# A decode step's backward pass: two MLP weight gradients and three wq gradients stored by GpSimd in three row pieces each

## The chip, the cores and the metric

The kernel runs on one core of a Trainium2 chip. A core has TensorE (PE, with its weight loads shown apart as PEld), VectorE (DVE), ScalarE (ACT), GpSimd (POOL) and SyncE (SP), and sixteen DMA engines that move data between HBM and SBUF for all of them. The metric is the device time of one execution in microseconds; less is better.

## The reference

One token of a pre-norm decoder block, and its gradients. With `xn = layernorm(x)`, the output is `x + attention(xn) + mlp(xn)`:

```
q = xn @ wq                      # 32 heads of 128; wq is 640 x 4096
p = softmax(q . k_cache / sqrt(128))   # 32 heads, 8192 cached positions
o = p . v_cache ; attention = o @ wo   # wo is 4096 x 640
mlp = (silu(xn @ w1) * (xn @ w3)) @ w2 # w1, w3: 640 x 1728, w2: 1728 x 640
```

All is bf16 outside. Wanted are the output and the gradients with respect to x, k_cache, v_cache, wq, wo, w1, w3 and w2. With a single token every weight gradient is an outer product, as large as the weight itself; so are the gradients of the caches: for each head two matrices of 8192 x 128, 2 MB each, are read (K, V) and two of that size are written (dK, dV). In all 151 MB are read and 151 MB written.

## The kernel before

**Tiling.** A cache matrix of one head lies in SBUF as 128 partitions of 64 positions x 128, so each partition holds one contiguous row of 16 KB. Ten such slots (`NSLOT`, L92) are all there is. K and V of a head are loaded into slots, used, overwritten in place by dK and dV (`outer`, L464 to L475, on DVE), stored from the same slot, and the slot then takes the next load. "KV" below means these loads and stores.

**Order.** The program is written out by hand in the order in which each engine runs it (`manual_schedule`). `head(h)` (L746) goes through a head's transposes, scores, softmax and weighted sums, and through the outer products of the head before it; the heads come in eight groups of four (`NG`, `GH`).

**Queues.** SP issues all loads and stores of the caches, in one order: `load_next` (L122) takes the next pending load when a slot is free, and `store` (L477) issues a store and then a load. SP waits at each for whatever that transfer needs, and everything behind it waits too. GpSimd issues the weights of the attention (`load_group`, L109: a wq tile of 128 x 5 x 512 and a wo tile of 128 x 4 x 640, 640 KB each, three of each in turn) and nearly all weight gradients. A transfer that GpSimd issues goes out on another queue (q0) than SP's (q1).

**The MLP** (`mlp`, L557) runs once, before head 2 (`MLP_AT`). Its weights lie in four of the ten slots. The gradients of w1 and w3 are made in place, the first four fifths of each (`wa`, 128 x 4 x 1728, 1728 KB) in a slot of its own: stored at L665, after which L666 gives the slot back and L667 issues the next KV load into it. The last fifth (`wb`) is stored at L676.

**The attention weights' gradients.** In the group after, `fin_wo` (L518, one call) and `fin_wq` (L524, five calls in the course of heads 1 and 2 of the group) turn the tiles of group g into gradients. `store_group` (L505) stores them; then `load_group(g + 3)` refills the wq tile that was just stored, so its load waits until the store has landed. How the rows of the 128 partitions are divided over transfers is this:

- wo of groups 0 to 6, and wq of groups 0 and 6: one transfer of 128 rows, by GpSimd.
- wq of groups 1 to 5 (`split`): rows 0 to 4 and rows 5 to 125 by GpSimd, rows 126 and 127 by SP (`fifo`).
- wo and wq of the last group, 7: rows 0 to 67 by SP, rows 68 to 72 and 73 to 127 by GpSimd. This is after all KV stores have been issued.

A row is 5,120 bytes of wq or wo (five pieces of 1,024 bytes, or four of 1,280, in HBM), and 13,824 bytes of the MLP's `wa` (four of 3,456).

**The end.** After the last head, the outer products and gradients of the last group, two small rows and the gradient of x (L842 to L868) are stored by SP.

Of the kernel before, what the change touches and what calls it, by code (L numbers as in the profile page):

```python
# [16 lines left out]
P = 128  # L17
# [4 lines left out]
def kernel(  # L22
# [22 lines left out]
    nc = tc.nc  # L45
# [8 lines left out]
    GH = 4  # L54
    NG = H // GH
    GW = GH * DH
# [23 lines left out]
    dwq_v = out_4.rearrange("(ci p) n -> p ci n", p=P)  # L80
    dwo_v = out_5.rearrange("(h p) c -> p h c", p=P)
# [9 lines left out]
    NA = NC - 1  # L91
# [12 lines left out]
    def fifo(out_, in_):  # L104
        nc.sync.dma_start(out_, in_)
# [3 lines left out]
    def load_group(g, eng):  # L109
        wq_g = wpool.tile([P, NC, GW], BF16, name="wq_g", tag="wq_g")  # L110
        eng.dma_start(wq_g[:], wq_v[:, :, g * GW:(g + 1) * GW])
        wo_g = wpool.tile([P, GH, D], BF16, name="wo_g", tag="wo_g")
        eng.dma_start(wo_g[:], wo_v[:, g * GH:(g + 1) * GH, :])
        grp[g] = dict(wq=wq_g, wo=wo_g)
# [7 lines left out]
    def load_next():  # L122
        if not pending or len(free_slots) < lag[0]:
            return
        kind, h = pending.pop(0)
        t = free_slots.pop(0)
        fifo(t[:], (kc if kind == "K" else vc)[h])
        kv_tiles[(kind, h)] = t
# [84 lines left out]
    def t_tile():  # L213
        t = kt_tile()
        return t[:].rearrange("p k w -> p (k w)").bitcast(BF16)
# [286 lines left out]
        for hh in range(GH):  # L502
            out_row(G_["od_bf"][:, hh, 0:1], G_["wo"][:, hh, :])

    def store_group(g, dst, t, split=False):  # L505
        if split:
            for lo, hi in ((0, 5), (5, 126)):
                nc.gpsimd.dma_start(dst[lo:hi], t[lo:hi])
            fifo(dst[126:P], t[126:P])
            return  # L510
        if g < NG - 1:
            nc.gpsimd.dma_start(dst, t[:])
            return
        fifo(dst[0:68], t[0:68])
        for lo, hi in ((68, 73), (73, P)):
            nc.gpsimd.dma_start(dst[lo:hi], t[lo:hi])

    def fin_wo(g):  # L518
        G_ = grp[g]
        for hh in range(GH):  # L520
            nc.vector.tensor_scalar(G_["wo"][:, hh, :], g_bc[:], G_["od"][:, hh, 0:1], None, ALU.mult)
        store_group(g, dwo_v[:, g * GH:(g + 1) * GH, :], G_["wo"])

    def fin_wq(g, ci):  # L524
        G_ = grp[g]
        wq_g, dqb = G_["wq"], G_["dqb"]
        nc.vector.scalar_tensor_tensor(wq_g[:, ci, :], wq_g[:, ci, :], 1.0, dqb, ALU.mult, ALU.mult,  # L527
                                       accum_out=dxa[:, ci, g:g + 1])
        nc.vector.tensor_scalar(wq_g[:, ci, :], dqb, xn_col[:, ci:ci + 1], None, ALU.mult)
        if ci == NC - 1:  # L530
            store_group(g, dwq_v[:, :, g * GW:(g + 1) * GW], wq_g, 1 <= g <= 5)
            grp.pop(g)
            if g + 3 < NG:
                load_group(g + 3, nc.gpsimd)
# [22 lines left out]
    def mlp():  # L557
# [57 lines left out]
        for ci in range(NC):  # L615
            for e in range(2):
                lo, hi = max(ci * P, e * DHALF), min((ci + 1) * P, (e + 1) * DHALF)
# [34 lines left out]
        for wi in range(2):  # L652
            wa, wb = ((w1a, w1b), (w3a, w3b))[wi]
            dv = (dw1_v, dw3_v)[wi]
            for f0 in range(0, F, FA):
                fn = min(FA, F - f0)
                T3 = t_tile()[:, 0:NA * fn].rearrange("p (c f) -> p c f", f=fn)
                nc.vector.tensor_tensor(T3, wa[:, :, f0:f0 + fn],
                                        bc_sb[:, wi, f0:f0 + fn].unsqueeze(1).to_broadcast([P, NA, fn]), ALU.mult)
                for i in range(fn // RX):  # L660
                    nc.tensor.matmul(dx_acc[:, 0:NA, :], lhsT=ident_bf[:], rhs=T3[:, :, RX * i:RX * (i + 1)],
                                     start=False, stop=True, skip_group_check=True)
            for ci in range(NA):
                nc.vector.tensor_scalar(wa[:, ci, :], bc_sb[:, wi, :], xn_col[:, ci:ci + 1], None, ALU.mult)
            nc.gpsimd.dma_start(dv[:, 0:NA, :], wa)  # L665
            free_slots.append((mA, mB)[wi])  # L666
            load_next()  # L667
            for f0 in range(0, F, FB):
                fn = min(FB, F - f0)
                T2 = t_tile()[:, 0:fn]  # L670
                nc.vector.tensor_tensor(T2, wb[:, f0:f0 + fn], bc_sb[:, wi, f0:f0 + fn], ALU.mult)
                for i in range(fn // RX):
                    nc.tensor.matmul(dx_acc[:, NA, :], lhsT=ident_bf[:], rhs=T2[:, RX * i:RX * (i + 1)],
                                     start=False, stop=True, skip_group_check=True)
            nc.vector.tensor_scalar(wb, bc_sb[:, wi, :], xn_col[:, NA:NC], None, ALU.mult)
            nc.gpsimd.dma_start(dv[:, NA, :], wb)  # L676
# [7 lines left out]
    def side_k(h):  # L684
        g, hh = divmod(h, GH)
        if hh == 1 and g > 0:
            fin_wq(g - 1, 0)
        elif hh == 2 and g > 0:
            fin_wq(g - 1, 3)
        elif hh == 3 and g + 1 < NG:  # L690
            prep_do(g + 1, 1)

    def side_m(h):
        g, hh = divmod(h, GH)
        if hh == 0 and g > 0:
            fin_od(g - 1)
        elif hh == 1 and g > 0:
            fin_wq(g - 1, 1)
        elif hh == 2 and g > 0:
            fin_wq(g - 1, 4)  # L700
        elif hh == 3 and g + 1 < NG:
            prep_do(g + 1, 2)
            prep_do(g + 1, 3)

    def side_v(h):
        g, hh = divmod(h, GH)
        if hh == 0 and g > 0:
            fin_wo(g - 1)
        elif hh == 1 and g > 0:
            fin_wq(g - 1, 2)  # L710
        elif hh == 2 and g + 1 < NG:
            prep_new(g + 1)
            prep_do(g + 1, 0)
        elif hh == 3 and g + 1 < NG:
            prep_cm(g + 1, hd[h]["m"][:, 324:324 + 4 * GH])
# [109 lines left out]
    for h in range(H):  # L825
        if h == MLP_AT:
            outers_a(h - 1)
            outers_b(h - 1)
            mlp()
        head(h)  # L830
        if h < 2:
            nc.gpsimd.tensor_copy(gate[:], hd[h]["rdot"][:])
            load_group(h + 1, nc.gpsimd)
    outers_a(H - 1)
    outers_b(H - 1)
    fin_od(NG - 1)
    fin_pe(NG - 1)
    fin_wo(NG - 1)
    for ci in range(NC):
        fin_wq(NG - 1, ci)  # L840
# [58 lines left out]
```

## Time and profile before

| what | value |
|---|---|
| time, median of 3 executions | 728.35 us (727.81 to 730.17) |
| time of the profiled execution | 730.06 us |
| its span, first to last instruction | 728.3 us |
| PE / DVE / ACT / POOL busy | 600.8 / 460.1 / 375.7 / 35.0 us |
| bytes moved, mean rate | 303.53 MB, 417 GB/s |
| q1 (issued by SP) | 22,022 packets, 277.14 MB |
| q0 (issued by GpSimd) | 6,272 packets, 25.56 MB |
| a KV transfer, issue to landing, median | 26.0 to 30.9 us |

The profile is one execution. "Busy" is the time in which an engine ran an instruction; the time of issuing transfers is not in it, except GpSimd's. The slices cut the span into forty equal parts and give each one's busy share in tenths. In the list of queues each line has packets, megabytes and the share of sixteen DMA engines' time. In windows, a line gives a stretch, then per engine the busy time and the number of instructions, the granted TensorE clock, the mean share of the DMA engines that was busy, and the rate in GB/s; overlaps of a few ns between packets can put the share at 1.01. In a table of waits, a line names who waited, for whom, how long in all, how often, and the longest. A timeline's line has start, duration, engine and instruction, and in brackets the idle time before it and what ended it.

### The profile page before, as it was taken

How to read it: one execution, taken by the hardware profiler on the slowest of the kernel's cores; microseconds unless marked ns; L12 is line 12 of the kernel's file. 1: busy time of each engine (PE TensorE's matmuls, PEld its weight loads, DVE VectorE, ACT ScalarE, POOL GpSimd, SP SyncE). 2: the span in 40 equal slices, each digit the busy share in tenths (PEclk: the TensorE clock that was granted, in tenths of full speed). 3: DMA queues.
4: the chain of work that ended last, by engine and by line, in shares of the span. 5: the costliest groups of instructions: out<-in, count | busy, mean ns of one | idle time of the engine just before them, and what ended most of it. 6: DMA issues, size and time to landing. Idle time of an engine off the chain costs nothing.

```text
span 728.3 us, 12951 instructions
## 1 busy us (share of the span) xinstructions
PE 600.8 (82%) x5193; PEld 375.6 (52%) x5193; DVE 460.1 (63%) x811; ACT 375.7 (52%) x727; POOL 35.0 (5%) x52
## 2 busy tenths in 40 slices
PE   3989589999999999877986889878896987988840
PEld 2547456665566556544554555445563555644520
DVE  4169646677767886767556746556755665677482
ACT  3640736665666656544554546455562555645410
POOL 0010110000100000000010000000000000000000
PEclk9996799999999999999999989999998999999975
DMA  9999999999999999999999999999999999999996
GB/s 347 398 409 424 427 428 428 413 427 425 418 409 429 427 426 424 423 429 422 425 425 427 431 420 427 421 427 432 410 428 424 428 425 422 429 424 430 429 415 239
DMA packets 28358, 303.53 MB, mean 417 GB/s; under 512 B 3481, under 2 KB 5532, under 8 KB 11658
## 3 DMA queue, kind: packets, MB, share of 16 engines
q1 hardware_dynamic: 22022, 277.14, 90.4%
q0 software_dynamic: 6272, 25.56, 8.8%
q8 instruction: 41, 0.67, 0.4%
q14 instruction: 19, 0.16, 0.1%
q10 hardware_dynamic: 4, 0.00, 0.0%
HBM read 151.34 MB, written 151.34 MB: 416 GB/s over the span
## 4 chain that ended last, share of the span: by engine, by line
DMA 57%; PE 33%; DVE 5%; ACT 2%; issue 1%; SPq 0%; ACTq 0%; DVEq 0%
DMA out_dram<-kv 30%; DMA kv<-in_A_k_cache_dram 18%; PE pT L318 15%; DMA kv<-in_A_v_cache_dram 7%; PE sA L339 4%; PE X L433 3%; PE dA L339 3%; DVE kv L466 2%; PE m L356 2%; DMA wo_g<-in_A_wo_dram 2%; ACT KT L320 1%; PE gu_ps L562 1%; PE dh_ps L573 1%; DVE side L257 0%; PE pT L266 0%
## 5 line engine op out<-in xcount | busy, mean ns | idle before, releaser
L320 ACT COPY KT<-pT 128x512 f32<-128x512 f32 x512 | 287.7, 587 | 230.9 <-PE pT L318 210.3
L318 PE MATMUL pT<-ident_f,kv 128*128 128x128 f32 x2048 | 306.6, 289 | 61.6 <-DMA kv<-in_A_k_cache_dram 29.9
L318 PEld LDWEIGHTS pT<-ident_f,kv 128*128 128x128 f32 x2048 | 236.2, 148 | 155.1 <-issue 59.6
L466 DVE TENSOR_TENSOR kv<-qd,U 128x4096 bf16<-128x4096 bf16 x64 | 146.0, 2283 | 0.0
L466 DVE TENSOR_TENSOR kv<-qd,P 128x4096 bf16<-128x4096 bf16 x64 | 143.5, 2283 | 0.0
L433 PE MATMUL X<-kv,Z 128*32 128x512 bf16 x1024 | 93.5, 402 | 1.8 <-DVE Z L450 1.8
L339 PE MATMUL sA<-KT,qz 128*32 128x512 bf16 x512 | 83.9, 408 | 0.0
L339 PE MATMUL dA<-KT,qz 128*32 128x512 bf16 x512 | 83.3, 404 | 0.0
L416 DVE SCALAR_TENSOR_TENSOR U<-m,P 128x64 bf16<-128x64 f32 x32 | 7.5, 234 | 83.0 <-PE m L356 83.0
L382 DVE TENSOR_REDUCE mrow<-m 128x1 f32<-128x64 f32 x32 | 7.2, 223 | 75.1 <-PE m L356 75.0
L339 PEld LDWEIGHTS <-qz 128*32 128x32 bf16 x1024 | 29.6, 95 | 40.4 <-issue 37.7
L433 PEld LDWEIGHTS <-Z 128*32 128x32 bf16 x1024 | 32.4, 99 | 33.8 <-issue 5.7
L356 PE MATMUL m<-selc,KT 64*128 64x64 f32 x256 | 30.7, 243 | 8.6 <-ACT KT L346 8.6
L356 PEld LDWEIGHTS m<-selc,KT 64*128 64x128 f32 x256 | 21.7, 145 | 30.4 <-ACT KT L346 21.6
L376 ACT CAST qd<-pT 128x256 bf16<-128x256 f32 x32 | 11.9, 372 | 40.3 <-DVE kv L466 28.8
L389 DVE TENSOR_REDUCE negM<-m 128x1 f32<-128x128 f32 x32 | 9.3, 291 | 33.2 <-PE m L386 33.2
L527 DVE SCALAR_TENSOR_TENSOR wq_g<-wq_g,side 128x512 bf16<-128x512 bf16 x40 | 27.3, 682 | 0.0
L257 DVE SCALAR_TENSOR_TENSOR side<-wo_g,g_bc 128x640 bf16<-128x640 bf16 x32 | 26.2, 819 | 1.4 <-DMA wo_g<-in_A_wo_dram 1.1
L448 DVE SCALAR_TENSOR_TENSOR U<-m,P 128x128 bf16<-128x128 f32 x32 | 11.4, 355 | 15.8 <-PE m L446 15.8
L406 DVE RECIPROCAL rZ<-m 128x1 f32<-128x1 f32 x32 | 5.3, 166 | 24.2 <-PE m L400 24.2
L346 ACT COPY KT<-dA 64x512 f32<-64x512 f32 x32 | 18.6, 583 | 2.6 <-PE dA L339 2.6
L346 ACT COPY KT<-sA 64x512 f32<-64x512 f32 x32 | 18.6, 580 | 2.3 <-PE sA L339 2.1
(164 smaller groups left out, 377.4 us busy)
## 6 DMA issues: line engine op xcount, KB each, us to landing
out_dram<-kv SPq DMA_DIRECT2D x64, 2048.0 KB, 30.9
kv<-in_A_k_cache_dram SPq DMA_DIRECT2D x32, 2048.0 KB, 27.9
kv<-in_A_v_cache_dram SPq DMA_DIRECT2D x32, 2048.0 KB, 26.0
wq_g<-in_A_wq_dram POOLq DMA_DIRECT2D x7, 640.0 KB, 13.5
wo_g<-in_A_wo_dram POOLq DMA_DIRECT2D x7, 640.0 KB, 19.6
out_dram<-wo_g POOLq DMA_DIRECT2D x7, 640.0 KB, 15.6
kv<-in_B_w_dram SPq DMA_DIRECT2D x2, 1728.0 KB
out_dram<-kv POOLq DMA_DIRECT2D x2, 1728.0 KB, 23.2
```

Source lines behind the costliest of these rows:

```text
L257: nc.vector.scalar_tensor_tensor(junk[:], G_["wo"][:, hh, :], 1.0, g_bc[:], ALU.mult, ALU.mult, accum_out=G_["do"][:, hh:hh + 1])
L318: nc.tensor.transpose(pT[:, k * P:(k + 1) * P], W3[:, 4 * c + k, :], ident_f[:])
L320: nc.scalar.copy(KT[:].rearrange("p k w -> p (k w)"), pT[:])
L339: nc.tensor.matmul(S_[kind][q:q + QW, :], lhsT=S_["qz"][:, o:o + QW], rhs=KTb[c][:, par, :], start=(c0 == 0 and par == 0), stop=(c0 == NCH ...
L346: nc.scalar.copy(XS[0:QH].rearrange("p k w -> p (k w)"), S_.pop(kind)[0:QH, :])
L356: nc.tensor.matmul(S_["m"][:, b0:b0 + 4 * J].rearrange("p (x c k t) -> p k x c t", x=4, k=4, t=2)[:, k], lhsT=XS[0:QH, k, :], rhs=selc[0:Q ...
L376: nc.scalar.copy(qd[:].rearrange("p a d -> p (a d)"), hd[h].pop("ps_r"))
L389: nc.vector.tensor_reduce(S_["negM"][:], S_["m"][:, 2 * J:2 * J + P], AX.X, ALU.max, negate=True)
L433: nc.tensor.matmul(xg["X"][q:q + QW, :], lhsT=Z[:, o:o + QW], rhs=W[:, N4 * i:N4 * (i + 1)], start=(slot == 0 and i < 4), stop=(slot == NS ...
L448: nc.vector.scalar_tensor_tensor(S_["U2"][:], S_["V"][:, 0:J].unsqueeze(2).to_broadcast([P, J, 2]), S_["m"][:, OC + NS:OC + NS + 1], S_["P ...
L466: nc.vector.tensor_tensor(dst[:, lo * DH:hi * DH].rearrange("p (j a b) -> p j a b", a=DH // 2, b=2), vec.rearrange("p (a b) -> p a b", b=2 ...
L527: nc.vector.scalar_tensor_tensor(wq_g[:, ci, :], wq_g[:, ci, :], 1.0, dqb, ALU.mult, ALU.mult, accum_out=dxa[:, ci, g:g + 1])
```

## The change

`store_group` is replaced by `store_rows`, which takes a list of row counts: each count is one transfer of so many rows, by GpSimd, or by SP where the count is negative. The two large MLP gradient stores (L665) now go through it too.

```diff
-    def store_group(g, dst, t, split=False):
-        if split:
-            for lo, hi in ((0, 5), (5, 126)):
-                nc.gpsimd.dma_start(dst[lo:hi], t[lo:hi])
-            fifo(dst[126:P], t[126:P])
-            return
-        if g < NG - 1:
-            nc.gpsimd.dma_start(dst, t[:])
-            return
-        fifo(dst[0:68], t[0:68])
-        for lo, hi in ((68, 73), (73, P)):
-            nc.gpsimd.dma_start(dst[lo:hi], t[lo:hi])
+    def store_rows(dst, t, pieces):
+        lo = 0
+        for n in pieces:
+            eng = nc.gpsimd if n > 0 else nc.sync
+            eng.dma_start(dst[lo:lo + abs(n)], t[lo:lo + abs(n)])
+            lo += abs(n)
+        assert lo == P
+
+    CYCLE = ((5, 120, 3), (14, 105, 9), (8, 105, 15), (2, 120, 6), (11, 105, 12))
+    LAST = (-68, 5, 55)
+    DWO_ROWS = {NG - 1: LAST}
+    DWQ_ROWS = {2: CYCLE[2], 3: CYCLE[3], 4: CYCLE[4], NG - 1: LAST}
 
     def fin_wo(g):
...
-        store_group(g, dwo_v[:, g * GH:(g + 1) * GH, :], G_["wo"])
+        store_rows(dwo_v[:, g * GH:(g + 1) * GH, :], G_["wo"], DWO_ROWS.get(g, (P,)))
...
         if ci == NC - 1:
-            store_group(g, dwq_v[:, :, g * GW:(g + 1) * GW], wq_g, 1 <= g <= 5)
+            store_rows(dwq_v[:, :, g * GW:(g + 1) * GW], wq_g, DWQ_ROWS.get(g, (P,)))
...
-            nc.gpsimd.dma_start(dv[:, 0:NA, :], wa)
+            store_rows(dv[:, 0:NA, :], wa, CYCLE[wi])
```

So the gradient of w1 leaves in 5, 120 and 3 rows and that of w3 in 14, 105 and 9; the wq gradients of groups 2, 3 and 4 in 8, 105 and 15, in 2, 120 and 6, and in 11, 105 and 12; those of groups 1 and 5 in one transfer. The five two-row transfers by SP are gone. The last group is stored as before. PE, DVE and ACT run the same instructions in the same order; GpSimd has 62 instructions in its list in place of 57, SP 144 in place of 149.

## The prediction

> **What bounds the kernel.** I read the slices and queues of the page first, then stretches of the run, then the waits of SP's queue, then the trace's records of single packets and completion counts. The page:
>
> ```profile
> span 728.3 us, 12951 instructions
> ...
> DMA  9999999999999999999999999999999999999996
> ...
> q1 hardware_dynamic: 22022, 277.14, 90.4%
> q0 software_dynamic: 6272, 25.56, 8.8%
> q8 instruction: 41, 0.67, 0.4%
> ```
>
> The sixteen DMA engines are busy in every slice but the last; PE, the next, is at 82%. q1 is SP's traffic, q0 GpSimd's, q8 the fetching of instructions: 41 packets, 16 KB each. The windows (last two numbers of a line: DMA share, GB/s) show where the engines stop being full:
>
> ```profile
> 140.00:700.00 560.00, 486.08 (x4173) 299.78 (x4170) 365.19 (x599) 307.23 (x613) 23.61 (x29) 0.96 1.01 424
> 700.00:712.00 12.00, 1.99 (x14) 0.96 (x13) 10.78 (x19) 0.75 (x2) 1.29 (x2) 0.50 0.98 415
> 712.00:718.00 6.00, 0.93 (x3) 0.58 (x3) 3.45 (x17) 0.00 (x0) 1.34 (x2) 0.50 0.95 354
> 718.00:722.00 4.00, 0.00 (x0) 0.00 (x0) 0.00 (x0) 0.00 (x0) 0.00 (x0) 0.50 0.77 272
> 722.00:729.00 7.00, 0.00 (x0) 0.00 (x0) 0.00 (x0) 0.00 (x0) 0.00 (x0) 0.50 0.14 51
> ```
>
> So no byte moved earlier helps; what can be won is the ragged end, where some engines are done and others are not. SP waits accordingly, for stores that free a slot:
>
> ```profile
> SPq L105 <- DMA out_dram<-kv: 453.0, 50, 14.9
> SPq L105 <- DVE kv L466: 105.3, 16, 13.8
> ```
>
> The trace keeps the sixteen completion counts of each transfer, one per engine. For the last KV store (issued at 706.1) they came at:
>
> ```
> 712.9 713.0 713.1 713.1 713.4 715.0 716.6 719.4 720.3 721.0 722.2 722.4 723.4 724.0 724.4 727.4
> ```
>
> One engine is 3.0 us behind the next, the mean is 718.9, and the span ends 0.9 us after it. Who is who comes from the packet records (start, duration, size, queue; no engine). A packet starts 3 to 4 ns before its predecessor on the same engine ends, so from 140 us on the packets can be strung into sixteen chains:
>
> ```
> group           rows of the five split wq stores   16 KB fetches   idle 140-712 us   last KV packet ends
> front four      10, 10, 5, 5                       none            0.4 to 4.9        712.5 to 713.0
> slow one        5                                  none            none              720.7
> middle three    55 each                            none            under 0.8         712.7 to 716.0
> fetch eight     55 each                            4 or 5          under 0.1         718.9 to 727.0
> ```
>
> The slow one needs 627 ns a 16 KB packet, the others 614 to 622. The fetches go round the eight in turn, so one of the 41 makes a sixth on a single engine: the last one, at 703.0, is on the engine that ends at 727.0, and costs it 0.94 us and 0.4 more in the stretched packet behind. That engine is never idle between 140 and 727 us: its list of work is the time.
>
> **The change, part by part.** *Which engine gets which row.* A 5-row piece fell on five engines, a 121-row piece on the other eleven (its odd last packet of 3,072 bytes occurs 55 times, 11 engines by 5 stores), SP's 2 and 68 rows on two and four (besides a first count at issue, two and four more came). So k is the largest divisor up to 16; and since 5 and 11 fill a ring of sixteen, a cursor that goes on from piece to piece comes back to the same five each time, as it did. I number the ring so that the front four are 0 to 3 and the slow one 4, the cursor starting at 0; 5 to 7 are then the middle three. Placing each new piece so (120 and 105 rows on fifteen engines, 14, 9, 8, 15, 2, 6, 11, 12 one row each) gives in every triple 2 rows to engine 4, 8 or 9 to the rest:
>
> ```
> rows, all stores touched    0,1   2,3   4    5-7   8-12   13-15
> five wq gradients, before   10    5     5    55    55     55
> five wq gradients, after    41    41    22   41    41     42
> two MLP gradients, before   16    16    16   16    16     16
> two MLP gradients, after    17    17    4    17    17     16
> ```
>
> [...]
>
> *Price of a row.* wq: eight rows are ten packets of 4,096 bytes at 159 ns less 3.5 of overlap, 0.195 us a row. MLP: two packets of 6,912 bytes at 262 ns, 0.52 us a row. Both queues share the engine, so a row costs this wherever it stands.
> - Fetch eight: 14 rows less (13 on the last three), one MLP row more: -2.73 + 0.52 = -2.2, or -2.5. I take -2.3.
> - Slow one: +17 x 0.195 - 12 x 0.52 = -2.9; from 720.7 to 717.8. Its MLP relief may fall where it would have idled, and be worth nothing: +3.3, 724.0, still not last.
> - Front four: +6.6 (two) and +7.5 (two). After 690 they had idled 1.4, 4.3, 4.0 and 0.4 us for want of issued stores, which is filled first; and 0.6 us of filler packets (70 to 88 of 11 ns, for pieces that an engine has no part in) mostly goes. Their KV would end at 714.2 to 719.5 (713.0 + 7.5 - 0.4 - 0.6). Then come the untouched last rows by SP, 17 of wo and 17 of wq: 68 packets of 1,280 bytes (55 ns alone, 77 on average in this tail) and 85 of 1,024 (46): 7.1 to 8.7 us, and 0.5 for GpSimd's. But in the 30 us behind each split store the five engines left out by the 121-row piece show 4.2 to 5.1 us of stretched KV packets in all, the other eleven 0.7 at the median. With only engine 4 left out, I count 3.5 of this as gone. The worst of them then ends at 716.0 + 7.6 to 9.2 = 723.6 to 725.2; without that 727.1 to 728.7.
>
> *Queues.* GpSimd issues 62 instead of 57 rows, SP 5 fewer. A DMA costs GpSimd 0.5 to 0.9 us; it idles for tens of us before each store (39.9 at most), so nothing. The next wq load waited 28.0 us for the store, because the 2 rows on SP's queue land 20 us after their issue (262.6 to 282.5); GpSimd's own pieces land within 17.1, so the loads of g+3 start some 11 us earlier. They are needed a group later, and shift bytes only: bounds -0.3 to +0.3 (the stretch of KV packets beside such loads, 617 against 613 ns, on 30 packets an engine), taken as 0.
> *The slots of the MLP.* SP stands behind the two big MLP stores, since their slots take the next loads:
>
> ```profile
> 89.58 0.78 POOL L665 DMA_DIRECT2D out_dram<-kv  x1 [11.81 <-DVE kv L664]
> ...
> 97.90 0.76 POOL L665 DMA_DIRECT2D out_dram<-kv  x1 [5.98 <-DVE kv L664]
> ...
> 108.09 0.33 SPq L105 DMA_DIRECT2D kv<-in_A_v_cache_dram  x1
> 122.22 0.34 SPq L105 DMA_DIRECT2D out_dram<-kv  x1
> 125.88 0.33 SPq L105 DMA_DIRECT2D kv<-in_A_k_cache_dram  x1
> ```
>
> The loads at 108.09 and 125.88 go out as those stores land. A ninth row is two more packets between 611 ns packets of q1, 1.75 us, and two more issues up to 0.8: each store lands up to 2.5 us later. If the relieved engine was the last (one count of the second store comes 1.0 after the other fifteen), up to 1.0 earlier. Bounds -1 to +5; I take 0: all sixteen engines are busy in every microsecond from 10 to 145, and the store of 122.22, which waits for DVE, lands its first count at 128.7, later than a load issued 2.5 us late could start.
>
> *Sum.* The last engine goes from 727.4 to 725.1; the span from 728.3 to 726.0. The profiled run took 730.06, 1.76 outside the span, and is 1.7 above the median of 728.35; I carry the difference over: 726.0. [...]
>
> **The rivals.**
> 1. *The front four become the last, and it ends slower.* From the point where the stretch behind the stores does not go: their 7 us more and the tail of small packets end at 727.1 to 728.7 against 727.4, hence 728.1 to 729.7; I say 728.9. For it: one of them had only 0.4 us to spare, and the tail's packets ran at 77 instead of 55 ns. Against it: the four idled 10 us between 690 and 712.
> 2. *The MLP slots starve the queues*: the upper bound, 726.0 + 2.5 to 5, 728.5 to 731. For it: the shortest delays of SP's transfers, 6.5 us, are at 122 to 132, so little is queued there. Against it: no engine idles there.
> 3. *The relieved engine is not the slow one* (the change does not do what it says): my numbers follow from elimination, and the slow engine could as well be the ring's last, one before the front four, the cursor starting there. Then it takes the front four's +7.5: 720.7 to 728.2, and the time is 729.2. [...] Against it: the fetch engines are eight, and only with the slow one at 4 are they a half of the ring.
>
> **The numbers.** What can be told from no change is 0.3%, 2.2 us. Forecast 0.46 (own range 724.5 to 727.0; faster 0.38, within 0.08); rival 1: 0.33 (within 0.24, slower 0.09); rival 2: 0.09 (slower 0.08, within 0.01); rival 3: 0.12 (faster 0.02, within 0.03, slower 0.07). Faster 0.40, within 0.36, slower 0.24. The range takes in rival 1 and most of 2 and 3: 724.0 to 730.2.
>
> **What would show it.** Right: the last counts of the last KV store closer together (now 14.5 us), the latest some 2.3 us earlier; the front four's no longer first; SP's loads at 108.1 and 125.9 no more than 2.5 us later. Rival 1: SP's last wq rows land after the last KV store (724.8 against 727.4 now). Rival 2: DMA share under 1.0 between 100 and 140 us. Rival 3: an engine with 627 ns packets lands last. What would make it wrong altogether: a cursor that does not start where it did, so that each triple relieves another engine.

## The result, and the profile after

The changed kernel takes 731.69 us (median of 22 runs, 727.39 to 735.26), the kernel before 728.93 (22 runs, 727.12 to 732.0): a ratio of 1.0037, interval 1.0021 to 1.0052. It is slower by more than can come from chance, where 726.0 was forecast. The profiled execution took 733.86, 1.76 of it outside its span; it lies 2.2 us above its kernel's median, and the profiled one of before (730.06) 1.1 above its own, so a difference of 2 us or so between single counts of the two says little. The page of the changed kernel:

```profile
span 732.1 us, 12936 instructions
...
DMA  9999999999999999999999999999999999999994
GB/s 354 396 408 424 423 427 419 355 428 425 413 424 432 428 425 421 426 430 429 423 424 431 430 421 426 426 429 427 423 429 428 430 428 429 428 429 429 429 423 157
...
q1 hardware_dynamic: 21962, 277.09, 89.8%
q0 software_dynamic: 6128, 25.61, 8.7%
q8 instruction: 41, 0.67, 0.4%
```

The row of GB/s in the kernel before:

```profile
GB/s 347 398 409 424 427 428 428 413 427 425 418 409 429 427 426 424 423 429 422 425 425 427 431 420 427 421 427 432 410 428 424 428 425 422 429 424 430 429 415 239
```

Two numbers stand out. The eighth, for 128 to 146 us, is 355; in the kernel before it was 413. The last is 157, where it was 239: the end has become longer and emptier. The windows show that end in the changed kernel (last two numbers of a line: DMA share, GB/s):

```profile
140.00:700.00 560.00, 488.10 (x4157) 300.18 (x4156) 366.13 (x599) 306.61 (x612) 23.26 (x30) 0.95 1.01 427
700.00:712.00 12.00, 2.08 (x14) 1.18 (x14) 10.25 (x29) 0.58 (x1) 2.26 (x4) 0.50 1.00 426
712.00:718.00 6.00, 0.66 (x3) 0.28 (x2) 1.12 (x5) 0.00 (x0) 0.37 (x1) 0.50 0.91 347
718.00:722.00 4.00, 0.00 (x0) 0.00 (x0) 0.00 (x0) 0.00 (x0) 0.00 (x0) 0.50 0.63 225
722.00:733.00 11.00, 0.00 (x0) 0.00 (x0) 0.00 (x0) 0.00 (x0) 0.00 (x0) 0.50 0.16 55
```

Between 140 and 700 us the engines are as full as before, and move 427 GB/s in place of 424. What was lost was lost ahead of 140 and behind 712. The completion counts of the last transfers say who is late at the end:

```
                                         before                        after
last KV store, earliest ... latest       712.9 ... 724.4 727.4         712.4 ... 724.0 726.0
last wq gradient, SP's 68 rows           721.7 722.5 723.3 724.8       725.7 726.0 727.0 731.0
last result row (fin_bf)                 725.0                         731.2
```

The last KV packet is 1.4 us earlier than before, as the change meant; but SP's 17 wq rows on each of the front four are now last, by 5.0 us. SP's issue of these rows has changed too, first before, then after:

```profile
713.62 0.28 SPq L105 DMA_DIRECT2D out_dram<-wq_g  x1
```

```profile
710.76 9.88 SPq L509 DMA_DIRECT2D out_dram<-wq_g  x1
```

The issue took 9.88 us in place of 0.28, and no packet of these rows started before 721.2. SP's wo rows, the store ahead of them, landed on the four engines at 717.8, 718.3, 723.4 and 727.4 (717.8 to 720.1 before). So two engines had none of these rows to move for some 3 us; the last of the four lost nothing by it, it was late with its wo rows already. The prediction has no such wait, and what holds the issue the runs don't show.

The other loss is at the slots of the MLP. First GpSimd's issues, then SP's:

```profile
88.02 2.36 POOL L509 DMA_DIRECT2D out_dram<-kv  x3 [11.80 <-DVE kv L664]
...
96.35 1.85 POOL L509 DMA_DIRECT2D out_dram<-kv  x3 [5.39 <-DVE kv L664]
```

```profile
111.01 0.33 SPq L105 DMA_DIRECT2D kv<-in_A_v_cache_dram  x1
120.26 0.34 SPq L105 DMA_DIRECT2D out_dram<-kv  x1
130.66 0.33 SPq L105 DMA_DIRECT2D kv<-in_A_k_cache_dram  x1
131.04 0.42 SPq L105 DMA_DIRECT2D out_dram<-kv  x1
```

The two stores were issued 1.5 us earlier than before, and yet the loads that wait for them go out 2.9 and 4.8 us later (108.09 and 125.88 before). SP's store of 120.26 has landed on 14 of 16 engines by 131, nothing else is in SP's queue until the load of 130.66, and the engines run dry. The stretch ahead of it, then the dry one, then the same five us in the kernel before:

```profile
108.00:128.00 20.00, 19.89 (x171) 12.41 (x171) 13.39 (x27) 13.20 (x28) 0.00 (x0) 1.00 1.00 420
128.00:133.00 5.00, 4.58 (x51) 2.95 (x52) 2.11 (x5) 2.81 (x8) 0.00 (x0) 1.00 0.68 239
```

```profile
128.00:133.00 5.00, 4.46 (x44) 2.74 (x47) 3.73 (x9) 3.19 (x7) 0.00 (x0) 1.00 1.02 433
```

A share of 0.68 in place of a full one over 5 us is 1.6 us of all sixteen engines. SP's own waits over the whole run fit this: it waits more for the landing of stores.

```profile
SPq L105 <- DMA out_dram<-kv: 492.7, 56, 16.7
SPq L105 <- DVE kv L466: 84.9, 14, 10.5
```

That is 40 us more for stores than before (453.0), and 20 less for DVE (105.3); between 84 and 135 us alone it is 43.9 us in place of 32.5.

So there are two suspects: the split MLP stores (theory 1: the slots come free later, the queue runs dry, and an engine-microsecond that is lost there is lost) and the front four's tail (theory 2: they got 31 to 36 wq rows more and kept the last group's 17 wo and 17 wq rows).

### The profile page after: what moved, and what is told of

It reads as the page before. It is cut to its first block, busy times and chain, and to the rows that moved or that the text cites. A ratio compares the mean times of both kernels' runs of the same rounds, so it can differ in the third digit from the quotient of the medians.

```text
span 732.1 us, 12936 instructions
## 1 busy us (share of the span) xinstructions
PE 602.6 (82%) x5193; PEld 376.4 (51%) x5193; DVE 460.2 (63%) x811; ACT 376.1 (51%) x727; POOL 37.4 (5%) x57
## 4 chain that ended last, share of the span: by engine, by line
DMA 55%; PE 32%; DVE 6%; ACT 2%; issue 1%; SPq 0%; ACTq 0%; DVEq 0%
DMA out_dram<-kv 29%; PE pT L318 15%; DMA kv<-in_A_k_cache_dram 14%; DMA kv<-in_A_v_cache_dram 11%; PE sA L339 4%; PE dA L339 3%; PE X L433 3%; DVE kv L466 3%; PE m L356 2%; DMA wo_g<-in_A_wo_dram 2%; ACT KT L320 1%; PE gu_ps L562 1%; ACT KT L346 1%; DVE wq_g L527 1%; DVE side L257 0%
## 5 line engine op out<-in xcount | busy, mean ns | idle before, releaser
L433 PE MATMUL X<-kv,Z 128*32 128x512 bf16 x1024 | 96.6, 412 | 1.8 <-DVE Z L450 1.8
L433 PEld LDWEIGHTS <-Z 128*32 128x32 bf16 x1024 | 33.2, 101 | 35.6 <-issue 8.7
L509 POOL DMA_DIRECT2D out_dram<-wq_g x15 | 11.0, 734 | 239.3 <-DVE wq_g L529 235.6
L509 POOL DMA_DIRECT2D out_dram<-wo_g x9 | 6.6, 737 | 278.1 <-DVE qz L363 240.5
```

The costliest lines, as they stand in the source:

```text
L433: nc.tensor.matmul(xg["X"][q:q + QW, :], lhsT=Z[:, o:o + QW], rhs=W[:, N4 * i:N4 * (i + 1)], start=(slot == 0 and i < 4), stop=(slot == NS ...
L509: eng.dma_start(dst[lo:lo + abs(n)], t[lo:lo + abs(n)])
```

## The experiments

Diffs are against the changed kernel. "(P,)" is a store in one transfer; where a text says "wq as before", groups 1 to 5 go as 5 and 121 rows by GpSimd and 2 by SP. Each ratio is to runs of the kernel before beside it.

**wq5, whole and last_whole: which part makes it slower.** wq5 undoes the MLP split, and splits all five wq gradients:

```diff
-    DWQ_ROWS = {2: CYCLE[2], 3: CYCLE[3], 4: CYCLE[4], NG - 1: LAST}
+    DWQ_ROWS = {1: CYCLE[0], 2: CYCLE[1], 3: CYCLE[2], 4: CYCLE[3], 5: CYCLE[4], NG - 1: LAST}
...
-            store_rows(dv[:, 0:NA, :], wa, CYCLE[wi])
+            store_rows(dv[:, 0:NA, :], wa, (P,))
```

> The changed kernel with the two MLP gradients whole again and the five wq gradients of groups 1 to 5 in the five triples (5,120,3), (14,105,9), (8,105,15), (2,120,6), (11,105,12). Slot theory (the split MLP stores land later, SP stands behind their slots, and all engines run dry at 128 to 132 us): SP's two loads behind the MLP stores go back to about 108 and 126, no microsecond between 100 and 140 has fewer than 15.8 busy engines, and the time falls by about 1.8 us against the changed kernel, to 730. Tail theory (the front four end last with SP's rows of the last group): those rows still land last, 2 to 5 us after the last KV store, so the time stays above the kernel before, 729.5 to 730.5. If the tail theory is wrong, the fetch engines' 14 rows less count, and it is 726.

728.74 us (727.75 to 730.96, 12 runs; 1.0005, interval 0.9993 to 1.0018): 2.95 less than the changed kernel. SP's loads go out at 107.28 and 125.25, and the DMA share from 128 to 133 us is 1.01. The last KV count comes at 723.1, 4.3 us earlier than in the kernel before; but SP's wq rows land at 719.7, 720.8, 724.1 and 725.0, and end the kernel. SP's issue of those rows took 5.35 us. The time is below what either theory gave (730, and 729.5 to 730.5). So the MLP split costs, and the front four end last also without it. How much of the 4.3 us is the wq split's work one profile can't say: in pieces_only below, with the wq rows as before, the last KV count is 724.8, 2.6 us earlier than in the kernel before.

The whole kernel stores the MLP gradients and wq groups 0 to 6 in one transfer each (`DWQ_ROWS = {NG - 1: LAST}` and the second edit of wq5).

> The changed kernel with no split except in the last group: MLP and wq gradients of groups 0 to 6 whole. Against the kernel before: fetch engines 15 wq rows less, -2.9 us; slow engine 35 more, +6.8, from 720.7 to 727.5 for its last KV packet; front four +5.8 and +6.8. Slot theory: no dry stretch at 128 to 132. Tail theory: SP's rows of the last group land last, about as in wq5 (one row less on the front four there and here), 729.5 to 730.5, and the slow engine does not matter. If relieving the slow engine is what counts, it ends last, near 728.5 + 0.7 = 729.2 against 726 for wq5.

730.70 (730.05 to 731.39, 12 runs; 1.0031, interval 1.002 to 1.0042), above the 729.2 that was expected where the slow engine counts. The last KV store's counts end with 720.4, 720.5, 721.0 and then 727.1: one engine is 6.1 us behind all others. I take it to be the slow one, which was expected at 727.5; the records don't name it. It has eight rows of everything here; if it is the slow one, leaving it out of rows is what both the 5-row pieces of before and the new pieces are worth.

last_whole keeps the whole change, but stores the last group's wo and wq gradients by GpSimd in one transfer each:

```diff
-    LAST = (-68, 5, 55)
+    LAST = (P,)
```

> The changed kernel with wo and wq of the last group stored whole by GpSimd (8 rows on each engine), in place of 68 rows by SP on the front four and 5 and 55 by GpSimd. Tail theory: the front four lose 10 rows twice, 3.9 us and the slow small packets; the last KV store's last count comes 1.2 us later (3 rows more, twice, on the fetch engines), at 727, and nothing lands after 728: time 731.7 - 731.0 + 727.5 = 728.2. Slot theory alone: the tail is not what ends the kernel, the rows only move 1.2 us onto the fetch engines, time 732.9.

729.23 (726.65 to 733.34, 12 runs; 1.0007, interval 0.9988 to 1.0026): 2.5 us less than the changed kernel. The last KV count is 725.5 and ends the kernel (span 726.7); the tail of the front four is gone, and with it the held issue. Both theories have their share so far: the MLP split some 2.9 us, the tail some 2.5. Neither run changes one thing alone: wq5 splits two wq gradients more, and last_whole gives the other engines three rows of each store more. Its profiled execution, with both MLP gradients in pieces, was not dry either (the second load went out at 127.16; DMA share 1.00 from 128 to 133 us).

**mlp_only: a run that tested something else.** The MLP split alone, wq as before. To bring the cursor back to where it stood I stored another MLP piece (L628 before) as 26 and 102 rows, taking 102 rows to be 17 on each of six engines.

```diff
+        store_rows(out_8[NBA * P:NFULL * P, :].rearrange("(fb p) c -> p fb c", p=P),
+                   w2b[:, 0:NFULL - NBA, :], (26, 102))
-            store_rows(dv[:, 0:NA, :], wa, CYCLE[wi])
+            store_rows(dv[:, 0:NA, :], wa, CYCLE[3 + wi])
```

> The kernel before with the two MLP gradients alone in three pieces, (2,120,6) and (11,105,12); the small store of 128 rows ahead of them goes as 26 and 102 rows, so that the ring's cursor stands where these two triples leave out the same engine. Slot theory: the second load behind an MLP store is issued at 129 to 131 instead of 125.9, all engines run dry for about 1.8 us, and the time is 730.5 to 731, 1.8 above the kernel before. Tail theory: the front four have one row more, 0.5 us, so they don't end last, and the time is that of before, 729. Both rest on the same engine sums: the last KV store's last count 0.5 later without the dry stretch.

738.72 (735.23 to 739.84, 6 runs; 1.0132, interval 1.0108 to 1.0155). The packets of the 102 rows are 15 of 5,120 and 14 of 3,840 bytes, which six equal shares can't give: that is seven rows (4 and 3) on fourteen engines, four on a fifteenth, none on the sixteenth. So the ring need not stand where I had meant it to, and by the packets it does not: the slow engine is here among the eleven that get 11 rows of each 121-row piece. Behind the odd 3,072-byte packets of these pieces stand KV packets of 611 to 614 ns in the kernel before, but here also one of 626, 621 and 619 ns in three of the five stores. Five times ten rows more at 0.195 us are 9.8 us. The slow engine had ended 6.7 us ahead of the last one before, at 720.7, so they take it to 730.5; the last KV count here is 731.9, in an execution of 735.23, the fastest of the six. That the median is 10.1 us above the kernel before is therefore not accounted for by these rows alone. The run says nothing of the MLP split.

**mlp_only2: the MLP split alone.** The MLP split as in the change, wq as before; the wo gradient of group 0 in 4, 60 and 64 rows turns the cursor, by the placing of the prediction, by the missing three.

```diff
-    DWO_ROWS = {NG - 1: LAST}
+    DWO_ROWS = {0: (4, 60, 64), NG - 1: LAST}
-    DWQ_ROWS = {2: CYCLE[2], 3: CYCLE[3], 4: CYCLE[4], NG - 1: LAST}
+    DWQ_ROWS = {**{g: (5, 121, -2) for g in range(1, 6)}, NG - 1: LAST}
```

> The kernel before, with the two big MLP stores in the changed kernel's pieces (5,120,3 and 14,105,9) and the wq gradients as before (5 and 121 by GpSimd, 2 by SP). The wo gradient of group 0 goes as 4, 60 and 64 rows, which brings the ring's cursor back to where it stood, so that the 5-row pieces fall on the same five engines as before. Slot theory: loads behind the slots near 111 and 130.5, a dry stretch of 1 to 2 us, and one MLP row more (0.5 us) on the engines that end last: 730.5 to 731.5. If the slots cost nothing: 729.4 (728.9 plus the row). If my reading of mlp_only (its 10 us come from the slow engine, which the moved cursor gave 11 rows of each wq store in place of 1) is wrong and the split MLP stores themselves cost them: near 738.

733.26 (730.7 to 735.36, 6 runs; 1.0061, interval 1.0041 to 1.0082): slower still than the changed kernel, and about 2 us above what theory 1 gave. The profiled execution was one of the fastest (730.77) and had no dry stretch (DMA share 1.00 from 128 to 133 us), though SP's loads went out late, at 113.25 and 127.74. So two more executions of it were profiled.

> The kernel of mlp_only2 once more, for a second profile: its first profile fell on an execution of 730.8 without a dry stretch, while the other executions went up to 735.4. If the dry stretch behind the w3 slot makes the slow ones: an execution of 732.5 or more shows the engines dry for 1 us or more between 128 and 133, and one near 731 does not. If a slow execution shows none, the split costs it elsewhere, and the packets' stretch or the end of the kernel must show it.

> As mlp_only2_b, a third profile: a dry stretch of 1 us or more in an execution of 732.5 or more, none in one near 731, if the slot's late release makes the slow ones.

They fell on either side, as theory 1 has it: 730.91 and 734.56. Around the second load, first mlp_only2_b, then mlp_only2_c:

```profile
128.00:133.00 5.00, 4.46 (x39) 2.88 (x35) 4.47 (x11) 3.08 (x9) 0.00 (x0) 1.00 1.02 415
```

```profile
128.00:133.00 5.00, 4.46 (x51) 2.60 (x48) 2.64 (x4) 3.20 (x7) 0.00 (x0) 1.00 0.75 272
```

The longer one is dry for a quarter of 5 us, 1.2 us; the other is not. Their issues by SP, in the same order:

```profile
122.99 0.34 SPq L105 DMA_DIRECT2D out_dram<-kv  x1
128.86 0.33 SPq L105 DMA_DIRECT2D kv<-in_A_k_cache_dram  x1
```

```profile
121.02 0.34 SPq L105 DMA_DIRECT2D out_dram<-kv  x1
130.28 0.33 SPq L105 DMA_DIRECT2D kv<-in_A_k_cache_dram  x1
```

In the dry execution the store went out at 121.02 and the load behind the slot at 130.28, and SP issued nothing between them; in the other they went out at 122.99 and 128.86. Of the 3.65 us between the two executions, the last KV count shows 1.2 (727.6 and 728.8), but SP's last wq rows 4.2 (727.3 and 731.5): the front four lose more by it than the gap. Why they do, the runs don't say. Nor is the dry stretch all that the split costs here: the two executions without one are still 2.1 and 1.7 us above the kernel before beside them.

**pieces_only and turns10: what makes the slot late.** The kernel before, with the MLP stores in pieces that, by the placing of the prediction, give every engine its eight rows and leave the cursor where it was; wq as before in both:

```diff
-            store_rows(dv[:, 0:NA, :], wa, CYCLE[wi])
+            store_rows(dv[:, 0:NA, :], wa, (16, 96, 16))          # pieces_only
+            store_rows(dv[:, 0:NA, :], wa, (5, 11, 5, 11, 96))    # turns10
```

> The kernel before, with the two big MLP gradient stores in pieces of 16, 96 and 16 rows: every engine keeps its eight rows and the cursor of the ring is not moved, so only the number of pieces and of issues differs. Slot theory, if the late landing comes from three pieces (two more issues of 0.6 us and two more turns in the queue): SP's loads behind the slots go out near 110 and 129 in place of 108.1 and 125.9, the stretch around 130 runs dry for 1 us or more, time 730.0 to 731.0. If it comes from the ninth row on some engines or from where the rows lie: loads within 1.5 us of before, no dry stretch, time 728.6 to 729.2. Tail theory alone: no change, 728.9.

> The kernel before, with the two big MLP gradient stores in pieces of 5, 11, 5, 11 and 96 rows: every engine keeps its eight rows, and the cursor of the ring comes back to where it stood, but an engine that a piece leaves out gets filler packets in that piece, as many as the others have packets. So each engine goes through ten rows' turns of packets in place of the eight of pieces_only (16, 96, 16), two of them with 8-byte fillers. Theory that a filler waits for its turn behind a 16 KB packet of the other queue (0.6 us each, two a row): the loads behind the slots go out 2 to 3 us later than in pieces_only, near 112 and 129; 729.5 to 731.5. Theory that only rows with data count: loads near 109.5 and 126.5 as in pieces_only, 728.3 to 729.2.

pieces_only: 728.62 (727.23 to 730.27, 12 runs; 1.0004, interval 0.9991 to 1.0016). turns10: 730.04 (728.38 to 733.43, 12 runs; 1.002, interval 1.0007 to 1.0034). SP's loads, first pieces_only, then turns10:

```profile
109.40 0.33 SPq L105 DMA_DIRECT2D kv<-in_A_v_cache_dram  x1
...
126.48 0.33 SPq L105 DMA_DIRECT2D kv<-in_A_k_cache_dram  x1
```

```profile
113.56 0.33 SPq L105 DMA_DIRECT2D kv<-in_A_v_cache_dram  x1
...
128.92 0.33 SPq L105 DMA_DIRECT2D kv<-in_A_k_cache_dram  x1
```

Three pieces in place of one cost nothing that can be told; the same bytes on the same engines in unequal pieces delay the loads by another 4.2 and 2.4 us. (Some 1 us of each is that GpSimd's first issue came later in this execution, and turns10 issues two pieces more for each gradient.) What unequal pieces add in the traces is filler: the changed kernel has 96 packets of 8 bytes in GpSimd's queue at the MLP stores, the kernel before none. That is two, the packets of a row, for each row's depth and each engine left out (22 + 16 + 26 for 5, 120 and 3 rows, 4 + 14 + 14 for 14, 105 and 9): as many as the other engines have packets with data. On the one engine left out of the 120 rows they start at

```
95.4 96.0 96.0 96.7 97.3 97.9 98.5 99.1 99.7 100.4 101.0 101.0 101.6 102.2 102.8 103.5
```

nearly all of them some 0.62 us apart, which is a 611 ns packet of SP's queue and 9 ns of filler, less 3.5 of overlap. Being left out spared this engine the 262 ns of each packet with data, but not the turn behind SP's packet. The 14 of the 105-row piece start within 0.1 us, at 112.9 to 113.0, just behind the 4-byte packet that ends a transfer of SP's on that engine: there no packet of SP's stands between them. The pieces of the change take every engine through 1 + 8 + 1 = 10 rows' turns for w1 and 1 + 7 + 1 = 9 for w3, in place of 8. From the first piece's issue to the load behind it:

```
                 turns, w1 and w3     w1 slot    w3 slot    store before the second load
before           8, 8                 18.5       28.0       122.2
wq5              8, 8                 18.6       28.2       120.9
pieces_only      8, 8                 20.2       28.8       120.4
turns10          10, 10               23.3       30.2       122.5
last_whole       10, 9                22.6       27.9       123.3
mlp_only2        10, 9                22.6       28.4       123.1
mlp_only2_b      10, 9                22.8       28.6       123.0
mlp_only2_c      10, 9                22.5       32.0       121.0    dry
after            10, 9                23.0       34.3       120.3    dry
after_again      10, 9                22.3       32.7       120.4    dry
```

The first slot mostly follows the turns. The second does not only: with the pieces of the change it is 4 to 6 us late where SP's store went out at 120 to 121, and hardly late where that store went out at 123; without them a store at 120 to 121 does no harm. What sets 120 or 123 in an execution I have not followed further. turns10 was not dry in its profiled execution (DMA share 1.01 from 128 to 133 us), so its 1.4 us over pieces_only are measured, but not explained by that.

**dw3_whole and after_again: is it the second slot in the changed kernel.** dw3_whole stores the w3 gradient in one transfer, and splits four wq gradients, so that, by the placing of the prediction, the cursor ends where it did. after_again is the changed kernel, profiled once more.

```diff
-    DWQ_ROWS = {2: CYCLE[2], 3: CYCLE[3], 4: CYCLE[4], NG - 1: LAST}
+    DWQ_ROWS = {2: CYCLE[1], 3: CYCLE[2], 4: CYCLE[3], 5: CYCLE[4], NG - 1: LAST}
...
-            store_rows(dv[:, 0:NA, :], wa, CYCLE[wi])
+            store_rows(dv[:, 0:NA, :], wa, (CYCLE[0], (P,))[wi])
```

> The changed kernel with the w3 gradient stored whole and four wq gradients in pieces in place of three, which brings the ring's cursor to where it was at the end. The w1 gradient stays in 5, 120 and 3 rows. If the second slot's late release is what lets the queue run dry: the load behind it goes out near 127, no dry stretch at 130, 729.0 to 730.0, with the front four's tail still last. If the first slot's release matters as much, or the split stores cost in another way: 731.0 to 732.5, as the changed kernel.

> The changed kernel once more, for a second profile. Its runs lie between 727.4 and 735.3, the first profiled one at 733.9 with 1.8 us of dry stretch near 130 and the front four's tail 5 us behind the last KV packet. If the dry stretch and where it leaves the engines make that spread, a run near 729 shows little or none of it; a run of 732 or more shows it again. If the spread comes from the end of the kernel, the dry stretch is the same in both.

dw3_whole: 729.14 (727.08 to 731.1, 12 runs; 1.0004, interval 0.9992 to 1.0017), 2.55 less than the changed kernel, with the w1 gradient still in three pieces and its load at 111.63. Its second load and the stretch around it:

```profile
120.87 0.34 SPq L105 DMA_DIRECT2D out_dram<-kv  x1
127.73 0.33 SPq L105 DMA_DIRECT2D kv<-in_A_k_cache_dram  x1
```

```profile
128.00:133.00 5.00, 4.46 (x51) 2.68 (x50) 2.51 (x4) 3.20 (x7) 0.00 (x0) 1.00 1.01 391
```

With the store at 120.9 as in the changed kernel, but the load at 127.7, nothing runs dry. So what the MLP split costs in the changed kernel comes mainly with the second slot; dw3_whole also splits a fourth wq gradient, so the 2.55 us are not that alone. after_again took 731.31, and runs dry like the first profile:

```profile
128.00:133.00 5.00, 4.48 (x50) 2.85 (x51) 2.21 (x5) 2.86 (x7) 0.00 (x0) 1.00 0.77 263
```

That is 1.2 us in place of 1.6. Its last KV count is 725.4, and SP's wq rows land at 725.0, 725.0, 725.5 and 728.4: again one of the four is 3 us behind the rest and ends the kernel. That the spread between runs comes from the dry stretch alone is not shown by these two, only that both have it.

**before_last_whole, wq5_last_whole and wq5_wo_split: the tail.** before_last_whole is the kernel before with `LAST = (P,)`. wq5_last_whole is wq5 with `LAST = (P,)`; wq5_wo_split is wq5 with only the last wq gradient whole:

```diff
-    DWQ_ROWS = {1: CYCLE[0], 2: CYCLE[1], 3: CYCLE[2], 4: CYCLE[3], 5: CYCLE[4], NG - 1: LAST}
+    DWQ_ROWS = {1: CYCLE[0], 2: CYCLE[1], 3: CYCLE[2], 4: CYCLE[3], 5: CYCLE[4], NG - 1: (P,)}
```

> The kernel before with the last group's wo and wq gradients stored whole by GpSimd in place of 68 rows by SP and 5 and 55 by GpSimd. Tail theory: before, the front four ended at 725.0, ahead of the KV packet at 727.4 of a fetch engine, and that engine now gets three rows of each more, 1.0 to 1.6 us: 729.7 to 730.5. If the 68-row stores cost something of their own wherever they stand, as last_whole's gain alone could also be read: 726.5 to 728.5.

> MLP stores whole, five wq gradients in three pieces, and the last group's wo and wq gradients whole in place of 68 rows by SP and 5 and 55 by GpSimd. Tail theory: the four engines with SP's 17 and 17 rows no longer end the kernel; the others get three rows of each more, 1.6 us, on a last KV packet that ended at 723.1 in wq5: end of the span 725 to 726, time 727.5 to 728.5 (wq5: 728.7). If the front four's tail did not matter in wq5, the added rows make it slower: 729.5 to 730.5.

> As wq5_last_whole, but only the last wq gradient whole; the last wo gradient stays 68 rows by SP and 5 and 55 by GpSimd. Tail theory: the front four lose nine of the 17 wq rows, some 3 us of the 725.2 at which their tail ended in wq5, the others gain three wq rows, 0.7 us, on 723.1: end of the span 724 to 725, time 726.7 to 727.7. If the tail of the front four did not matter: 729.0 to 729.7.

before_last_whole: 729.24 (726.84 to 730.45, 10 runs; 1.0009, interval 0.9996 to 1.0022). It falls between the two expectations: no gain, as theory 2 has it where the front four are not last, but the loss is 0.3 us, inside the interval, and not 1; its last KV count is 727.8. wq5_last_whole: 727.09 (725.67 to 729.85, 12 runs; 0.9981, interval 0.9967 to 0.9994). wq5_wo_split: 726.23 (725.21 to 727.2, 9 runs; 0.9968, interval 0.9958 to 0.9979), faster than both kernels. Its end:

```profile
700.00:712.00 12.00, 2.75 (x15) 1.47 (x15) 9.26 (x33) 0.59 (x1) 2.17 (x3) 0.50 0.99 419
712.00:718.00 6.00, 0.00 (x0) 0.00 (x0) 0.27 (x1) 0.00 (x0) 0.00 (x0) 0.50 0.88 353
718.00:722.00 4.00, 0.00 (x0) 0.00 (x0) 0.00 (x0) 0.00 (x0) 0.00 (x0) 0.50 0.39 155
722.00:733.00 11.00, 0.00 (x0) 0.00 (x0) 0.00 (x0) 0.00 (x0) 0.00 (x0) 0.80 0.01 2
```

The last KV count comes at 723.3, SP's last wo row at 722.3 and the last result row at 722.5: the fetch eight, the front four and the small rows end within 1 us, and behind 722 there is nearly nothing. The same edit, the last group whole, that gains nothing in the kernel before gains 1.65 us over wq5, where the front four have been made the last. These runs take away SP's last rows and, in wq5_wo_split, their held issue (5.35 us in wq5) together: how the tail's cost divides between the rows and the wait for their issue is not shown. The issue took 4.2 to 9.9 us in after, after_again, wq5, dw3_whole and mlp_only, and 0.3 us in the other kernels that have it.

## Why the prediction was wrong

Two steps failed: that the front four's stretched packets would go, and that the MLP slots cost nothing. Rivals 1 and 2, given 0.33 and 0.09, both happened.

- *Fetch eight, -2.3:* right in sign and about in size, but medians show it, not single counts. The last KV count moved by -1.4 in the changed kernel, by -3.0 if the 1.6 us of dry stretch are taken off, and by -4.3 in wq5; but it moved by -2.6 in pieces_only as well, where the wq rows are those of before. With the last group whole in both, the five split wq gradients gain some 2 us (before_last_whole 1.0009, wq5_last_whole 0.9981), where 13 rows less at 0.195 us are 2.5. The placing was less exact: by the chains strung along the change's rows, the eight engines with four or five fetches are three of the ring's places 5 to 9, all of 10 to 12 and two of 13 to 15, not 8 to 15. Their rows differ by one at most, so it cost nothing.
- *Slow one, -2.9 and not last:* the place was right. In the changed kernel the fillers of the three big wq pieces, which by the placing only the engine at place 4 gets, stand between KV packets of 615 to 676 ns, while around nearly all other fillers they take 611. So rival 3 did not happen. The records don't name engines.
- *Which engine gets which row:* the divisor and the running cursor held for the stores of the change: 96 fillers at the MLP stores, the number that the placing gives, 30 odd packets of 3,072 bytes, fifteen engines by two 105-row stores, and the slow engine the one left out by all three big wq pieces. The divisor did not hold for the 102 rows of mlp_only, which lay on fifteen engines where it gives six. Those were single rows of 1,280 bytes, the change's stores have four or five segments a row; what decides between the two was not shown.
- *Front four:* the step that failed is "I count 3.5 of this as gone". Over all engines the stretch of KV packets above 611 ns did fall, from 97.9 to 56.9 us between 141 and 712. On the front four, by the strung chains, it fell from 6.8 and 9.6 to 1.0 and 1.2 us on two, from 7.4 to 3.3 on the one with five fetches of 8 KB (q14, not named in the prediction), but only from 8.2 to 6.7 on the one with eight such fetches. The forecast end of 723.6 to 725.2 plus the dry stretch is 725.2 to 726.8, and three of SP's four wq counts are 725.7, 726.0 and 727.0; that they fit is in part luck, since their packets waited until 721.2 for an issue that the forecast does not have. The fourth, 731.0, is past even the end without the credit (728.7 to 730.3 with the dry stretch), and was late before that wait mattered: its wo rows landed at 727.4. I take it to be the engine that kept its stretch; the small packets of the tail can't be followed far enough to show it. Rival 1 happened, and last_whole measures it: 2.5 us, net of what three rows more cost the other engines.
- *The MLP slots, "I take 0":* the second step that failed. The late landing was seen in kind (up to 2.5 us; it became 2.9 and 4.8, for the first slot since the engines left out take their turns too: 23.0 us from issue to load in place of 18.5), but its price was taken from engines that were busy in the kernel before, and from a store of 122.22 whose first count came at 128.7. In the changed kernel that store went out at 120.26 and had landed on most engines when the load of 130.66 came: dry for 1.6 us. Rival 2 happened as well; dw3_whole and wq5 measure 2.55 and 2.95 us, each with one or two more wq gradients split.
- *Queues, 0:* the wq loads did start earlier: after the store of some 330 us GpSimd waited 14.2 us in place of 35.6. What that is worth was not tried by itself; no run speaks against 0.
- *Sum:* 731.69 less 2.95 (MLP) and 2.5 (tail) is 726.2, where the forecast was 726.0. That they meet so closely is in part luck: the two runs are not single terms, since wq5 also splits two gradients more, and the forecast started from 728.35, the median of three executions, where 22 gave 728.93. But wq5_wo_split, which has neither loss, measures 726.23. The gain was there; a term taken as nothing and a credit of 3.5 us that came only in part ate it and 2.8 us more.
- *One transfer or pieces:* equal pieces of the MLP stores leave the time as it was (pieces_only, 1.0004), unequal ones cost (turns10 1.002, mlp_only2 1.0061), and unequal pieces of the wq gradients gain 0.3% once the tail fits them (wq5_wo_split, 0.9968).

## What to carry to other kernels

On this kernel, whose sixteen DMA engines moved 424 GB/s between 140 and 700 us at a share of 1.01, a split that gave the late engines fewer rows did gain (wq5_last_whole 0.9981, before_last_whole 1.0009), but not while the engines that got the rows were last (wq5, 1.0005). So work out the end of every group, with the small packets behind it, and move the last rows along with the first (wq5_wo_split, 0.9968). Don't split, in unequal pieces, a store whose buffer the next load waits for, without asking what else is in the queue: in turns10 the two loads went out 4.2 and 2.4 us later than in pieces_only, whose pieces are equal, and in the changed kernel an engine left out of a piece had its fillers some 0.62 us apart, between SP's packets. SP's queue, with nothing issued between 120.3 and 130.7 in the changed kernel, ran dry there, and in one of three profiled executions of mlp_only2. Profile more than one execution: the last KV count differed by 2.6 us between two kernels whose engines have the same rows (before and pieces_only). An unused microsecond of cover must be looked for in the changed order of work, since the transfer that covered it may go out earlier, too: here it went out at 120.26 in place of 122.22.

## What the hardware showed that was not expected

- An engine left out of a piece by GpSimd got a filler for each packet that the others had: 96 of 8 bytes (9 ns) at the changed kernel's MLP stores with their packets of 6,912, and 16 bytes (11 ns) at the wq stores with their packets of 4,096. On the engine left out of the 120 rows the fillers came some 0.62 us apart, with a 611 ns packet of SP's queue between them; on the one left out of the 105 rows, behind the end of a transfer of SP's, 14 fillers took 0.1 us.
- In mlp_only 102 rows of 1,280 bytes were spread as seven rows on fourteen engines and four on a fifteenth (15 packets of 5,120 bytes, 14 of 3,840), while 121 and 105 rows of five segments lay evenly on eleven engines (55 odd packets of 3,072 bytes in five stores, before) and on fifteen (30 in two, after).
- Executions of one kernel differ by whether a queue runs dry: 730.91 and 734.56 us for the same kernel, and all three dry executions that were profiled had the load behind the slot at 130.3 to 130.7.
- SP's issue of the last 68 wq rows took 0.28 us in the kernel before and 9.88 us in the changed one, where the store ahead of it landed on its four engines as late as 727.4 (before: 720.1).
- Behind the dry stretch the engines ended in step: the sixteen counts of the load behind the second MLP slot lie within 1.3 us in the changed kernel (138.3 to 139.6), against 2.8 us in the kernel before (134.0 to 136.8), and within 1.6 us in mlp_only2_c (138.2 to 139.8), which was dry, against 4.4 us in mlp_only2_b (136.6 to 141.0), which was not.
